# Another order of issue for a kernel that adds a long convolution and a gated unit, on one core

## The chip, the cores and the metric

One core of one Trainium2 chip. The metric is the device time in microseconds (us) of one execution, as the median of several runs. The core has five engines that run side by side, each through its own list of instructions in order: PE (TensorE, matmuls), DVE (VectorE), ACT (ScalarE), POOL (GpSimd) and SP (SyncE, which here only issues DMA transfers). An instruction waits until the results that it needs are there, and what stands behind it on its engine waits with it.

## What is computed

```python
x = A_q                                    # 2048 rows x 640 columns, bf16
xn = _layernorm(x, axis=-1)
return x + _A_ref(xn, A_k, A_v, A_shift_k, A_ssm_k, A_ssm_D) \
         + _B_ref(xn, B_w_gate, B_w_up, B_w_down)

# _A_ref(q, k, v, ...): a convolution over all 2048 rows
k_shift = sum of k_pad[:, t:t + S, :] * shift_k[:, 3 - t]   # four shifted copies of k
kv = k_shift * v
y = causal convolution of kv with ssm_k along the rows (by FFT), column by column
return q * (y + kv * ssm_D)

# _B_ref(x, ...): a gated unit, 640 -> 1728 -> 640
g, u = x @ w_gate, x @ w_up
return (sigmoid(g) * u) @ w_down
```

## The kernel before, in words

Two jobs share the engines.

**The gated unit** works on four tiles of 512 rows, numbered 0 to 3. A tile's normalised rows are turned (tile xnT; tiles 0 and 1 on PE, tiles 2 and 3 by a transposing DMA that reads them back from DRAM, `rec_tp`, L699). For each of 14 column groups fc of 128 columns, five matmuls of 128x512 make the gate and five the up half in PSUM (`rec_fc`, L770); ACT takes the sigmoid (L729, L735) and DVE multiplies (L732, L737) into hT; in some groups ACT copies the up half out first (L314, as hT<-g). Then `rec_down` multiplies hT with the down weights, seven matmuls of 128x320 at a time (L786), and DVE adds the result to the row accumulator acc (L798). Gate and up weights come in pieces called w3_0, w3_1 and so on (tile 3; even numbers gate, odd ones up, four column groups each, 640 KB) into four buffers; a piece can be loaded once the last matmul that reads the buffer's former piece is done (L378).

**The convolution** goes over the columns in two halves, each in five parts, so ten in all, as an FFT in matrix form. For a part, DVE makes kv (L470 to L488); stage 1 (L508, 32 small matmuls a group) and stage 2 (L528, 32 a group) transform on PE; ACT takes their results out of PSUM (L314, L317); DVE multiplies the spectra (`rec_prod`, L548 to L567; for seven of the parts two DMA transfers P<-S first swap the two halves of the partitions); stage 3 (L580, 8 matmuls a group) goes back into V. When five parts are done, stage 4 (`rec_st4`, L612) makes the half's rows, in four pairs u = 0 to 3 of two groups of 64 matmuls of 32x80; ACT or DVE evicts them, DVE multiplies them with the normalised rows, which a DMA has read back from DRAM into a buffer (L600; xq in half 0), and adds them to acc (L620, L621). Half 0 has two such buffers, so pair 2's rows are loaded when pair 1's addition is done. At the end SP stores acc in 24 transfers (L630).

The layer norm of tiles 1 to 3 is split: ACT makes sums and sums of squares (L646, L652), DVE the inverse root, ACT or DVE the rows (L685, L683).

**The order.** The program records 984 operations, each with what it reads and writes, and then emits them in the order of a list of numbers, `ORDER`; each engine's instruction list is what falls to it of that list. An operation that ACT and DVE can both do is done by ACT unless its number is in `ON_DVE`. Where a tile has several buffers, the order also decides which one it gets (`emit`). Nothing else sets the order.

The operations that the change and the prediction speak of, by number:

| Numbers | Operation |
|---|---|
| 384, 385; 377, 378; 391, 392; 398, 399 | stage 4 of half 0: the pairs u = 1, 0, 2, 3 |
| 579, 580; 572, 573; 586, 587; 593, 594 | stage 4 of half 1: the pairs u = 1, 0, 2, 3 |
| 388, 389 | DVE's product and addition of pair u = 1, half 0 |
| 390 | load of the rows for pair u = 2, half 0 |
| 437 | a DVE product of part 5 that waits for the transfers P<-S |
| 807, 841 | last up group of tile 2 that reads its xnT; the transposing load of tile 3 |
| 881, 893 | tile 3: gate of fc 3; up of fc 5 |
| 886, 887 | loads of the weights w3_2 and w3_3 |
| 45; 135, 136 | eviction of sT; norm of tile 1's rows, groups 2 and 3 |
| 139, 140, 141, 144 | norm of groups of rows of tiles 2 and 3 |
| 293; 820, 895 | eviction for the head of kt, half 1; copies of an up half to hT |
| 568, 570, 574, 575, 581, 582 | evictions of stages 3 and 4, half 1 |
| 960 to 967; 968 to 971; 972 to 983 | stores of rows 0 to 11; 12 and 13; 14 and 15 |

(Stores: in units of 128 rows.)

Of the kernel before, what the change touches and what calls it, by code (L numbers as in the profile page):

```python
# [42 lines left out]
def _dft_tables():  # L43
# [34 lines left out]


ORDER = [  # L80
    3, 5, 0, 8, 2, 7, 6, 42, 71, 12, 10, 13, 4, 11, 72, 14, 16, 1, 19, 73, 74, 75, 91, 76, 607, 86, 608, 18, 43, 96,
    77, 61, 97, 78, 79, 104, 62, 63, 64, 81, 20, 80, 92, 87, 17, 82, 98, 83, 643, 15, 88, 84, 85, 148, 99, 93, 89,
    645, 100, 149, 60, 625, 644, 58, 90, 94, 67, 626, 102, 101, 27, 150, 103, 613, 621, 66, 44, 615, 623, 65, 106, 68,
    154, 622, 57, 624, 614, 616, 617, 619, 105, 153, 609, 56, 59, 22, 611, 618, 108, 620, 599, 601, 610, 612, 600, 29,
    107, 109, 646, 602, 157, 32, 158, 648, 603, 605, 112, 647, 650, 113, 30, 151, 649, 651, 652, 635, 637, 111, 110,
    152, 604, 636, 31, 606, 638, 23, 155, 26, 631, 627, 633, 632, 25, 156, 24, 629, 118, 117, 634, 21, 639, 641, 120,
    628, 630, 640, 642, 667, 35, 114, 661, 116, 668, 671, 115, 662, 665, 121, 119, 36, 133, 122, 123, 127, 681, 124,
    673, 39, 37, 682, 128, 684, 674, 677, 134, 45, 129, 679, 135, 653, 680, 38, 654, 683, 663, 131, 657, 136, 658,
    664, 33, 47, 666, 125, 48, 675, 126, 137, 34, 54, 172, 655, 656, 676, 163, 678, 669, 164, 659, 162, 130, 660, 28,
    670, 165, 672, 689, 691, 167, 739, 741, 132, 166, 181, 690, 692, 168, 53, 740, 721, 182, 742, 831, 723, 743, 693,  # L90
    744, 159, 298, 160, 41, 171, 722, 745, 724, 698, 40, 161, 700, 730, 169, 49, 732, 699, 701, 702, 52, 183, 832,
    734, 731, 300, 50, 178, 51, 736, 170, 173, 733, 175, 179, 735, 180, 174, 685, 176, 737, 738, 138, 177, 195, 687,
    196, 725, 727, 299, 199, 305, 186, 185, 184, 201, 202, 197, 46, 686, 688, 187, 188, 198, 189, 200, 203, 301, 833,
    707, 709, 190, 791, 69, 192, 302, 55, 726, 712, 194, 728, 193, 708, 729, 141, 70, 710, 213, 227, 191, 714, 214,
    713, 711, 139, 303, 228, 715, 215, 95, 716, 703, 718, 229, 304, 218, 217, 233, 230, 204, 206, 231, 704, 140, 142,
    216, 219, 771, 705, 706, 220, 234, 221, 208, 694, 696, 224, 695, 232, 697, 205, 717, 226, 249, 254, 719, 753, 225,
    207, 143, 222, 746, 772, 755, 720, 250, 209, 251, 754, 210, 253, 223, 757, 756, 252, 211, 758, 767, 759, 260, 235,
    237, 239, 212, 255, 263, 760, 256, 768, 236, 238, 261, 262, 288, 264, 290, 763, 265, 266, 267, 269, 770, 270, 241,
    242, 257, 240, 243, 244, 258, 834, 268, 836, 747, 285, 407, 748, 146, 289, 306, 751, 245, 271, 273, 412, 275, 291,
    286, 786, 247, 788, 749, 259, 287, 761, 318, 272, 294, 145, 762, 246, 750, 319, 297, 248, 752, 320, 321, 764, 324,  # L100
    325, 410, 274, 322, 276, 279, 409, 765, 280, 292, 787, 323, 277, 278, 766, 315, 789, 769, 835, 293, 326, 838, 308,
    309, 837, 327, 295, 296, 317, 281, 307, 839, 840, 310, 777, 282, 790, 779, 811, 283, 316, 778, 312, 782, 284, 328,
    329, 340, 354, 330, 331, 784, 783, 780, 334, 785, 341, 144, 773, 332, 342, 812, 360, 358, 355, 333, 413, 356, 774,
    311, 792, 781, 359, 345, 775, 361, 776, 357, 336, 813, 313, 335, 822, 338, 362, 815, 824, 408, 337, 823, 314, 339,
    363, 825, 376, 793, 795, 344, 351, 353, 343, 346, 794, 411, 147, 796, 817, 404, 347, 352, 427, 814, 819, 365, 364,
    366, 826, 428, 406, 429, 431, 367, 418, 816, 370, 405, 433, 371, 432, 828, 867, 368, 414, 383, 818, 374, 434, 369,
    797, 820, 821, 375, 799, 372, 373, 827, 348, 349, 829, 350, 798, 830, 384, 385, 430, 417, 435, 800, 387, 416, 419,
    415, 806, 436, 866, 424, 801, 386, 425, 808, 802, 377, 426, 421, 378, 379, 380, 388, 389, 803, 449, 390, 804, 463,
    450, 420, 805, 464, 422, 807, 437, 453, 860, 809, 451, 381, 841, 810, 465, 467, 468, 423, 382, 469, 470, 439, 854,
    397, 861, 864, 438, 391, 392, 855, 440, 858, 872, 394, 452, 441, 466, 455, 874, 848, 456, 460, 454, 849, 852, 393,  # L110
    462, 443, 856, 442, 398, 399, 857, 461, 400, 444, 445, 859, 401, 471, 844, 457, 447, 458, 459, 472, 446, 448, 490,
    473, 842, 485, 486, 499, 500, 845, 847, 474, 843, 846, 487, 501, 503, 504, 476, 475, 477, 479, 505, 478, 850, 506,
    489, 862, 496, 502, 498, 480, 863, 851, 481, 865, 482, 507, 873, 508, 483, 886, 887, 488, 853, 491, 493, 877, 497,
    492, 494, 527, 875, 878, 876, 510, 512, 515, 484, 529, 528, 531, 533, 879, 880, 516, 509, 532, 881, 534, 511, 513,
    514, 883, 868, 519, 530, 870, 395, 882, 520, 926, 884, 535, 536, 571, 869, 521, 523, 927, 871, 901, 495, 903, 885,
    892, 537, 396, 928, 402, 522, 585, 894, 902, 906, 524, 904, 526, 592, 539, 578, 893, 525, 538, 517, 888, 549, 541,
    895, 896, 518, 905, 550, 890, 897, 551, 907, 555, 553, 899, 540, 898, 543, 544, 542, 900, 929, 556, 545, 554, 552,
    931, 930, 557, 558, 889, 932, 908, 403, 891, 559, 910, 547, 909, 911, 921, 561, 563, 912, 923, 922, 560, 914, 924,
    548, 913, 917, 546, 915, 564, 567, 562, 565, 566, 569, 933, 568, 570, 579, 580, 916, 925, 934, 919, 581, 582, 918,
    935, 583, 920, 572, 936, 584, 573, 574, 937, 940, 575, 586, 576, 577, 962, 587, 938, 589, 588, 590, 960, 942, 939,  # L120
    591, 967, 966, 593, 594, 941, 595, 963, 596, 944, 597, 598, 943, 945, 946, 947, 968, 948, 950, 971, 969, 949, 964,
    961, 952, 951, 965, 953, 975, 970, 972, 974, 973, 954, 955, 958, 979, 976, 956, 978, 977, 9, 957, 959, 980, 982,
    981, 983
]
ON_DVE = [
    101, 103, 133, 34, 140, 144, 820, 568, 582, 574, 589, 588, 595
]


# [798 lines left out]
```

## Time and profile before

| What | Value |
|---|---|
| Time of the kernel before, median of 3 runs | 256.01 us (255.62 to 257.51) |
| The profiled execution's own time | 256.55 us |
| Its span, from the first instruction to the last | 254.8 us |
| Granted TensorE clock | 0.998 |
| Matmuls of 128x512 (L770) | 520, 379 ns drawn for each |
| Matmuls of 128x320 (L786) | 448, 299 ns |
| Stage 4 (L612) | 1024, 203 ns |
| Idle of DVE before hT (L737), for PE | 17.7 us |
| Idle of ACT before sig (L735), for PE | 14.7 us |

A page of the profile gives each engine's busy time and its share of the span, then 40 equal slices of the span in which a digit is the busy share in tenths, then the DMA queues (packets, megabytes, share of the time of 16 DMA engines), the chain that ended last, and groups of instructions: line, engine, operation, out<-in, shape, count, busy us, mean ns of one, and the idle time ahead of them with what ended it. A timeline row has the start, the length, the engine, the line, the operation and the count, and in brackets the idle time before it and its releaser; "issue" is a wait for nothing that the profile shows. PEld are PE's weight loads, one for each matmul. Matmuls overlap, so the length drawn for one is longer than the step from one to the next.

### The profile page before, as it was taken

The page shows a single profiled execution, that of the slowest core. Times are in us where ns is not written, and L with a number is a line of the kernel's source. Part 1 is how long each engine was busy: PE and PEld are TensorE (multiplying, and loading weights), DVE is VectorE, ACT ScalarE, POOL GpSimd, SP SyncE. Part 2 cuts the span into 40 slices and gives each one's busy share as a digit, 9 for nine tenths or more (in the row PEclk, how much of TensorE's full clock was granted, in tenths as well). Part 3 has the DMA queues.
Part 4 walks back from the last instruction along what each step waited for, and adds up shares of the span by engine and source line. Part 5 has one row for each costly group of instructions (what it writes and reads, how often), then busy time and mean ns, then how long its engine had stood idle before and what let it go on. Part 6 is the DMA issues. An engine that isn't in the chain of part 4 may idle for free.

```text
span 254.8 us, 9455 instructions
## 1 busy us (share of the span) xinstructions
PE 241.0 (95%) x4231; PEld 145.1 (57%) x4231; DVE 199.8 (78%) x334; ACT 179.0 (70%) x263; POOL 0.7 (0%) x6
## 2 busy tenths in 40 slices
PE   7899999999999999999999999979999999898991
PEld 3654446664454657666564654656766465356770
DVE  5723347279999999999999999997999896878920
ACT  2737789975899986987798888846878895461300
POOL 1000000000000000000000000000000000000000
PEclk9999999999999999999999999999999999999999
DMA  6999999999989087698999757842127697000861
GB/s 179 335 250 317 246 256 135 143 184 192 153 196 290 5 227 187 95 144 118 166 226 234 194 163 190 100 111 59 35 55 233 148 300 214 3 3 23 191 156 53
DMA packets 91024, 41.44 MB, mean 163 GB/s; under 512 B 66656, under 2 KB 88104, under 8 KB 90664
## 3 DMA queue, kind: packets, MB, share of 16 engines
q1 hardware_dynamic: 90792, 40.52, 71.7%
q8 instruction: 33, 0.54, 0.9%
q10 hardware_dynamic: 192, 0.33, 0.4%
q14 instruction: 7, 0.06, 0.1%
HBM read 30.61 MB, written 5.24 MB: 141 GB/s over the span
## 4 chain that ended last, share of the span: by engine, by line
PE 59%; DVE 19%; ACT 9%; DMA 5%; issue 4%; ACTq 1%; SPq 0%; DVEq 0%
PE g L770 30%; PE g L786 16%; PE c L528 5%; DMA P<-S 3%; ACT jk L646 3%; PE c L612 3%; DVE kvt L488 2%; PE c L580 2%; DVE P L558 2%; ACT S L314 2%; DVE ta L475 2%; PE c L508 2%; DMA acc<-in_A_q_dram 2%; DVE tb L470 1%; PE c L750 1%
## 5 line engine op out<-in xcount | busy, mean ns | idle before, releaser
L770 PE MATMUL g<-xnT,w 128*128 128x512 bf16 x380 | 90.0, 379 | 0.9 <-DVE hT L737 0.7
L786 PE MATMUL g<-wd,hT 128*128 128x320 bf16 x448 | 66.6, 299 | 1.5 <-issue 0.8
L770 PEld LDWEIGHTS <-w 128*128 128x128 bf16 x380 | 35.0, 98 | 38.4 <-issue 1.2
L786 PEld LDWEIGHTS <-hT 128*128 128x128 bf16 x448 | 42.2, 98 | 19.0 <-issue 2.2
L314 ACT CAST S<-c 128x1024 bf16<-128x1024 f32 x40 | 39.7, 1027 | 3.9 <-PE c L528 3.8
L737 DVE TENSOR_TENSOR hT<-sig,g 128x512 bf16<-128x512 bf16 x32 | 21.9, 685 | 19.3 <-PE g L770 17.7
L770 PE MATMUL g<-xnT,V 128*128 128x512 bf16 x140 | 32.7, 379 | 0.0
L735 ACT ACTIVATE sig<-g 128x512 bf16<-128x512 f32 x32 | 19.3, 605 | 15.9 <-PE g L770 14.7
L798 DVE TENSOR_TENSOR acc<-g,acc 128x320 bf16<-128x320 f32 x32 | 15.5, 489 | 15.1 <-PE g L786 14.8
L528 PEld LDWEIGHTS <-Mt 64*128 64x128 f16 x1280 | 19.8, 95 | 5.4 <-issue 5.1
L314 ACT CAST T<-c 128x1024 bf16<-128x1024 f32 x20 | 19.8, 1020 | 3.6 <-PE c L508 3.5
L528 PE MATMUL c<-T,Mt 64*128 64x64 bf16 x1280 | 22.1, 190 | 0.0
L314 ACT CAST V<-c 128x1024 bf16<-128x1024 f32 x19 | 19.2, 1025 | 3.4 <-PE c L580 2.4
L488 DVE TENSOR_TENSOR kvt<-ta,vt 128x1024 bf16<-128x1024 bf16 x10 | 21.5, 2148 | 0.1
L770 PEld LDWEIGHTS <-V 128*128 128x128 bf16 x140 | 13.1, 98 | 14.7 <-issue 0.2
L317 ACT ACTIVATE T<-c 128x1024 bf16<-128x1024 f32 x20 | 20.3, 1039 | 0.8 <-PE c L508 0.8
L729 ACT ACTIVATE sig<-g 128x512 bf16<-128x512 f32 x18 | 10.9, 605 | 7.8 <-PE g L770 3.1
L475 DVE TENSOR_TENSOR ta<-ta,tb 128x1024 bf16<-128x1024 bf16 x20 | 13.8, 690 | 0.4
L470 DVE TENSOR_TENSOR tb<-kt,sT 128x1024 bf16<-128x1024 bf16 x20 | 13.7, 686 | 0.2
L561 DVE TENSOR_TENSOR S<-S 128x1024 bf16<-128x1024 bf16 x20 | 13.5, 687 | 0.3
L580 PEld LDWEIGHTS <-S 128*128 128x128 bf16 x160 | 10.9, 98 | 3.9 <-DVE S L567 1.2
L580 PE MATMUL c<-At,S 128*128 128x128 f16 x160 | 13.0, 219 | 0.0
(83 smaller groups left out, 241.2 us busy)
## 6 DMA issues: line engine op xcount, KB each, us to landing
w<-in_B_w_gate_dram SPq DMA_DIRECT2D x7, 640.0 KB, 5.7
w<-in_B_w_up_dram SPq DMA_DIRECT2D x7, 640.0 KB, 4.6
P<-S SPq DMA_DIRECT2D x14, 256.0 KB, 3.9
kt<-in_A_k_dram SPq DMA_DIRECT2D x8, 320.0 KB, 6.6
vt<-in_A_v_dram SPq DMA_DIRECT2D x8, 320.0 KB, 5.5
xnd<-xq SPq DMA_DIRECT2D x4, 640.0 KB, 4.7
ht<-in_A_ssm_k_dram SPq DMA_DIRECT2D x16, 96.0 KB, 4.3
wd<-in_B_w_down_dram SPq DMA_DIRECT2D x3, 480.0 KB, 8.6
```

Source lines behind the costliest of these rows:

```text
L314: fa = lambda: nc.scalar.copy(out=out_fn(), in_=in_fn())
L317: fa = lambda: nc.scalar.activation(out_fn(), in_fn(), ACT.Copy, scale=scale)
L470: dve(1024, 2, lambda: nc.vector.tensor_tensor(tl[c][:], sl(tl[kb], 3 - m), sh(m), ALU.mult) if c != o else nc.vector.tensor_tensor(tl[c]. ...
L475: dve(1024, 2, lambda: nc.vector.tensor_tensor(tl[a][:], tl[a][:], tl[c][:] if c != o else tl[c].rearrange("p b n j -> p n b j"), ALU.add) ...
L488: dve(1024, 1 if kt else 2, lambda: nc.vector.tensor_tensor(by_j(tl[o]) if kt else tl[o][:], tl[a].rearrange(form), sl(tl[vb], 0).rearrang ...
L528: nc.tensor.matmul(tl[c][:, b, 64 * kk:64 * kk + 64], lhsT=Mb[rows, k, 64 - 64 * r:192 - 64 * r], rhs=tl[T][rows, 2 * k + r].rearrange("p ...
L580: nc.tensor.matmul(o, lhsT=tl[S_][:, b, 0, j, :], rhs=Ab[:, 2 if zc else 0, :], start=True, stop=zc)
L735: act(512, lambda: nc.scalar.activation(tl[sg][:], pv(0), ACT.Sigmoid), r=[pk(0)], w=[(sg,)], alloc=[(sg, "sig")], pri=pri - 2000)
L737: dve(512, 1, lambda: nc.vector.tensor_tensor(hT[:, fc, :], tl[sg][:], pv(1), ALU.mult), r=[pk(1), (sg,)], w=[(hk, fc)], pri=pri - 2000)
L770: nc.tensor.matmul(tl[c][:], lhsT=w()[:, k, o:o + P], rhs=tl[X][:, k, :], start=(k == 0), stop=(k == NC - 1))
L786: nc.tensor.matmul(tl[pd[i]][:, 0:320], lhsT=hT[:, fc, t4 * P:(t4 + 1) * P], rhs=wd[:, fc, 320 * i:320 * i + 320], start=(fc == 0), stop=( ...
L798: dve(320, 1, lambda i=i, m=m, pd=pd: nc.vector.tensor_tensor(acc[:, m, 320 * i:320 * i + 320], tl[pd[i]][:, 0:320], acc[:, m, 320 * i:320 ...
```

## The change

Only the two lists change. The same 984 operations are issued in another order, and some operations change between ACT and DVE: 45, 135, 136, 139, 141, 293, 570, 575, 581 and 895 go to DVE; 140, 144, 568, 574, 582 and 820 go to ACT. The order came out of a search in which an engine's instruction fetch waits until the block ahead has come.

Nearly every line of `ORDER` differs; these are the ones around the operations in the table above.

```diff
 ORDER = [
...
-    797, 820, 821, 375, 799, 372, 373, 827, 348, 349, 829, 350, 798, 830, 384, 385, 430, 417, 435, 800, 387, 416, 419,
-    415, 806, 436, 866, 424, 801, 386, 425, 808, 802, 377, 426, 421, 378, 379, 380, 388, 389, 803, 449, 390, 804, 463,
-    450, 420, 805, 464, 422, 807, 437, 453, 860, 809, 451, 381, 841, 810, 465, 467, 468, 423, 382, 469, 470, 439, 854,
-    397, 861, 864, 438, 391, 392, 855, 440, 858, 872, 394, 452, 441, 466, 455, 874, 848, 456, 460, 454, 849, 852, 393,
-    462, 443, 856, 442, 398, 399, 857, 461, 400, 444, 445, 859, 401, 471, 844, 457, 447, 458, 459, 472, 446, 448, 490,
...
-    489, 862, 496, 502, 498, 480, 863, 851, 481, 865, 482, 507, 873, 508, 483, 886, 887, 488, 853, 491, 493, 877, 497,
-    492, 494, 527, 875, 878, 876, 510, 512, 515, 484, 529, 528, 531, 533, 879, 880, 516, 509, 532, 881, 534, 511, 513,
...
-    961, 952, 951, 965, 953, 975, 970, 972, 974, 973, 954, 955, 958, 979, 976, 956, 978, 977, 9, 957, 959, 980, 982,
...
+    797, 821, 828, 384, 430, 347, 349, 866, 385, 435, 799, 408, 350, 418, 387, 798, 827, 800, 386, 436, 424, 886, 416,
+    829, 806, 802, 426, 830, 417, 377, 388, 425, 463, 801, 415, 808, 804, 464, 437, 378, 389, 438, 380, 803, 439, 379,
+    805, 390, 449, 419, 807, 841, 450, 441, 854, 421, 391, 381, 392, 420, 809, 810, 440, 382, 443, 860, 855, 442, 393,
+    861, 451, 394, 467, 468, 858, 864, 422, 453, 397, 469, 470, 465, 423, 444, 868, 870, 850, 398, 452, 455, 399, 466,
...
+    873, 498, 865, 875, 869, 521, 510, 522, 527, 493, 877, 528, 876, 871, 509, 523, 881, 887, 883, 533, 529, 534, 879,
+    512, 492, 531, 878, 511, 513, 530, 515, 514, 516, 532, 880, 892, 494, 495, 882, 535, 536, 894, 517, 884, 893, 907,
...
+    971, 970, 949, 952, 968, 951, 953, 973, 975, 956, 974, 957, 972, 959, 981, 954, 955, 958, 982, 983, 980, 979, 976,
...
 ON_DVE = [
-    101, 103, 133, 34, 140, 144, 820, 568, 582, 574, 589, 588, 595
+    101, 103, 45, 133, 136, 135, 34, 139, 141, 293, 895, 570, 581, 575, 588, 589, 595
 ]
```

## The prediction

> **What bounds the kernel now.** I read the page first, then the groups by shape, then the order of PE's instructions, and last the timeline around PE's gaps. From the page, and from the groups by shape (the last line):
>
> ```profile
> span 254.8 us, 9455 instructions
> ...
> PE 241.0 (95%) x4231; PEld 145.1 (57%) x4231; DVE 199.8 (78%) x334; ACT 179.0 (70%) x263; POOL 0.7 (0%) x6
> ...
> PE   7899999999999999999999999979999999898991
> ...
> DVE  5723347279999999999999999997999896878920
> ...
> q8 instruction: 33, 0.54, 0.9%
> ```
> ```profile
> L612 PE MATMUL c<-V,Bt 32*32 32x80 bf16 x1024 | 10.6, 203 | 2.1 <-issue 2.1
> ```
>
> PE is busy in nearly every slice from 10 to 249 us, so the time is PE's work plus PE's waits, with DVE close behind (91.25 of the 94 us from 56 to 150). Queue 8 carried 33 packets, 0.54 MB: 16.4 KB each. PE has 8462 instructions (a weight load and a matmul, 4231 of each): 256 to a packet, 64 bytes each. So PE's program comes in blocks of 256. Stage 4 (L612) is densest: 128 instructions in about 0.63 us. There PE waits for "issue". The timeline, engine PE:
>
> ```profile
> 151.58 1.34 PE L612 MATMUL c<-V,Bt 32*32 32x80 bf16 x128
> ...
> 155.57 0.86 PE L612 MATMUL c<-V,Bt 32*32 32x80 bf16 x84
> 157.00 0.52 PE L612 MATMUL c<-V,Bt 32*32 32x80 bf16 x44 [0.56 <-issue]
> ```
> ```profile
> 165.20 0.27 PE L612 MATMUL c<-V,Bt 32*32 32x80 bf16 x20
> 166.21 1.06 PE L612 MATMUL c<-V,Bt 32*32 32x80 bf16 x108 [0.74 <-issue]
> ...
> 171.21 0.41 PE L508 MATMUL c<-Ft,kvt 32*128 32x64 f16 x32 [0.86 <-ACT xq L314]
> ...
> 174.94 0.54 PE L612 MATMUL c<-V,Bt 32*32 32x80 bf16 x46 [0.53 <-issue]
> ```
> ```profile
> 229.85 0.99 PE L786 MATMUL g<-wd,hT 128*128 128x320 bf16 x6 [0.83 <-issue]
> ...
> 233.30 0.80 PE L612 MATMUL c<-V,Bt 32*32 32x80 bf16 x77 [0.27 <-issue]
> ```
>
> Counted in PE's instructions these six stand at 4532, 5042, 5296, 5552, 7600 and 7856, all 176 to 180 past a multiple of 256, in the middle of groups whose data were there: block edges. (The 0.86 is put down to ACT, but its place is the same.) The idle adds up to 3.8 us. A shown end includes some 0.2 us of pipeline (a matmul is drawn 203 ns long while 64 of them start within 0.63), so the loss is 3.8 + 6 x 0.18 = 4.9 us. Between waits that follow each other lie 171.21 to 174.94 = 3.73 us and 229.85 to 233.30 = 3.45 us: the least time of a block. From 166.21 to 171.21 it was 5.0, with the transposing load of tile 3's rows in flight. The counter-example is the first line above: instructions 4020 to 4276, one whole block and nearly all stage 4, passed with a wait of 0.1 us; their packet ran from 150.37 to 151.44, before they were reached, because two L770 groups of 1.08 us stood ahead.
>
> **The change part by part.** Same operations, same buffers. Sums are made in the profiled execution, 256.55 us (span 254.8); the median of the runs is 256.01, and differences carry over.
>
> *Fetches.* With block edges at the same counts, the new order puts stage 4's pairs of half 0 at 4004-4260 (as before), 4364-4492 plus 4556-4684 (split), 4782-5038 and 5296-5552: the last two each fill one block. Laying the rows end to end (L770 1.08, L786 0.95, L528 0.47, L508 0.34, L612 0.63, 0.1 at each change of form) the blocks hold, in us:
> - 4276-4532 and 4532-4787: 4.3 and 4.6, over 3.73: 0.1 lost (0 to 0.7), where before lost 0.75.
> - 4787-5042: 1.3 of stage 4 alone. At best the stream is ahead by the L770 and L786 groups in front (2.0), and the edge at 5042 costs 3.45 - 3.3 = 0.1. At worst it is not ahead and the transposing load is in flight: 5.0 - 1.3 = 3.7. That load is issued after the last tile-2 L770 group, 14 instructions before this block, so I take 2.4, nearer the worst. Before: 0.92 + 1.02 at these two edges.
> - 5296-5552: the same shape, but 6.4 us of work lie before it and that load has landed: 0.2 (0.1 to 2.4). Before 0.7.
> - The last three (7344 on): 3.3, 3.05, 3.05 against 2.7, 3.0, 3.95 before: 1.0 (0.95 to 1.8). Before 1.45.
>
> Sum 3.7 (1.15 to 8.6) against 4.9: **-1.2** (-3.75 to +3.7).
>
> *Changes of form.* L508, L528 and L612 come in 41 runs instead of 43; each costs 0.1 going in and out: **-0.4**.
>
> *ACT to DVE at 45-50 us.* sT's eviction and two norms of tile 1 go to DVE. PE waited there: one L786 group starts at 48.18, the next at 49.69, 0.56 over its 0.95. ACT was full (9.78 of 40-50), DVE half empty (5.01) with 1.7 to 2.3 us idle between evictions, which hides 0.82 + 2 x 0.44; uncovered, that would be 1.7. **-0.5** (-0.56 to 0). In the full DVE stretch the exchanges cancel: two norms in (0.88), two out (0.88), kt's head in (0.40), one hT copy out (0.69).
>
> *Stores.* SP issues its last stores back to back:
>
> ```profile
> 241.84 10.78 SPq L630 DMA_DIRECT2D out_dram<-acc  x19
> ```
>
> 0.57 us each, up to 252.6, and the span ends 2.2 later. One store of rows 12-13 now goes ahead of the last twelve: **-0.5** (-1.3 to 0).
>
> *What gets later.* (a) Stage 4's third pair starts about 4 us earlier and needs a row load that two DVE operations release; one of them now stands behind a product that waits for the P<-S load. In before the load landed 8.8 us after the first pair's end; the new order gives 10.35 us of PE work, less what DVE loses: **+0.5** (0 to 1.5). (b) The weights w3_3 were issued at 190.06, long before use. Now their buffer is free only when the L770 group of fc 3 (gate) ends, 5.2 us of PE work ahead of their first use by fc 5 (up). The weight loads' line has
>
> ```profile
> DMA to landing us min/median/max: 4.5/5.3/9.2
> ```
>
> so 0.2 to issue plus 5.3, less 5.2: **+0.3** (0; 3.3 at the 8.3 us that this load took beside its twin). The wait at 218.99 (0.69, for an hT product that stands behind the P<-S load on DVE) stays; its order there is the same.
>
> Sum: -1.2 - 0.4 - 0.5 - 0.5 + 0.5 + 0.3 = -1.8: 254.75 in the profiled execution, **254.2** from the median.
>
> **The rivals.**
>
> *The filled blocks run free.* As 4020-4276 did, if the stream keeps its lead: loss 1.15 instead of 3.7, 254.2 - 2.55 = 251.6. For it: the two pairs fit their blocks to within six instructions. Against it: the transposing load.
>
> *The fetch is no limit, so nothing is won there.* If the six waits are queue waits that merely show up there, they move along: 254.2 + 1.2 = 255.4. Against it: six of six at one remainder. [...]
>
> *No lead (slower).* Where the stream reaches a stage-4 block only as PE does, its 1.3 us cover nothing: 3.7 at 5042, 2.4 at 5552, the other ends with them, 8.6 in all: 254.2 + 4.9 = 259.1. It ends above before once the two blocks cost 4.4 together instead of 2.6. For it: the block ahead, 4.6 us, is under the 5.0 seen with a load in flight, and could use up the lead.
>
> *w3_3 lands late.* At 8.3 us, 254.2 + 3.0 = 257.2; it decides from a landing of 7.1. Against it: nothing else is issued beside it.
>
> **How the numbers follow.** The forecast 0.44, free blocks 0.28, no limit 0.10, no lead 0.10, w3_3 late 0.08. 254.2 is the likeliest's; its own range is 253.0 to 255.6, from the ends of its small terms. The range 251.4 to 257.4 takes in free blocks and late weights and leaves out no lead and the far edge of free blocks. A measurement of this kernel tells about 1% (2.6 us) from no change: faster by more than that is free blocks and a little of the forecast, 0.34; slower is most of no lead and a little of late weights, 0.12; within it 0.54.
>
> **What would show it.** PE's waits for issue: none in the split pair (4364-4684), one of 2 us or more just after the pair at 4782-5038, next to none after 5296-5552, three small ones after 228 us. ACT's wait of 0.39 at 49.69 gone. PE's wait for w at the first fc 5 (up) group under 0.5. The last store's issue half a us nearer to PE's end. I am wrong if PE's waits for DVE or ACT grow by over 1 us between 56 and 150, where DVE has 2.7 us to spare, or if the edges have moved.

## The result, and the profile after

The changed kernel takes **256.28 us** (median of 20 runs, 253.32 to 258.92) where the kernel before, run beside it, takes 257.37 us (median of 20). The ratio is **0.9935, 95% interval 0.9908 to 0.9961**: 0.4 to 0.9% faster. (The ratio is formed from the fast runs alone and leaves out six of the changed kernel's 20, 257.25 to 258.92 us with a mean clock of 0.986 to 0.993; that is why the medians of all 20 lie only 1.1 us apart.) In a second series the medians were 254.38 us (12 runs) and 256.21 us (23 runs), ratio 0.9925 (0.9897 to 0.9953). The execution that was profiled was the slowest of the 20 (258.92 us, with PE's clock at half speed for a while), so times of it are not compared with those of before as they stand.

Its page:

```profile
span 257.1 us, 9426 instructions
...
PE 241.5 (94%) x4199; PEld 146.9 (57%) x4231; DVE 202.2 (79%) x338; ACT 177.0 (69%) x259; POOL 0.7 (0%) x6
...
PE   7999999999999999999999899599989999899993
...
PEclk9999999999999999999999999869999999999999
...
q8 instruction: 33, 0.54, 1.0%
```

PE's row has a hole in the 26th slice (163 to 166 us), and the clock's row, full in the kernel before, dips in the slices 26 and 27. (32 of the 4231 matmuls are missing from this record; the weight loads are complete.) The timeline of the changed kernel, engine PE, shows the hole: stage 4's pair u = 2 (128 matmuls of L612) and what follows.

```profile
161.82 1.23 PE L612 MATMUL c<-V,Bt 32*32 32x80 bf16 x128
162.98 0.31 PE L786 MATMUL g<-wd,hT 128*128 128x320 bf16 x1
166.43 5.37 PE L786 MATMUL g<-wd,hT 128*128 128x320 bf16 x20 [3.15 <-issue]
```

The pair runs without a stop, one matmul of the next group starts, and then PE stands for 3.15 us for nothing that the profile shows: this is PE instruction 5040, a block edge. The 20 matmuls behind it take 5.37 us; the same 20 take 2.89 us where the clock is whole (below). The table by stretches of the same profile (the column behind POOL is the granted clock) says why:

```profile
160.00:163.00 3.00, 3.00 (x141) 1.99 (x139) 2.93 (x5) 1.43 (x2) 0.00 (x0) 1.00 0.47 131
163.00:166.40 3.40, 0.28 (x7) 0.07 (x1) 3.33 (x7) 2.20 (x3) 0.00 (x0) 0.75 1.17 121
166.40:168.00 1.60, 1.57 (x6) 0.88 (x7) 0.54 (x1) 0.00 (x0) 0.00 (x0) 0.50 1.03 263
```

The clock falls to 0.50 while PE waits and stays there for 6.8 us in all. The edges behind 228 us answer to those of before at 229.85 and 233.30: one visible wait, in the middle of a stage-4 group.

```profile
239.95 0.30 PE L612 MATMUL c<-V,Bt 32*32 32x80 bf16 x29
240.88 0.98 PE L612 MATMUL c<-V,Bt 32*32 32x80 bf16 x99 [0.63 <-issue]
```

At the end, SP's 24 stores, first in the kernel before and then in the changed one:

```profile
234.66 17.96 SPq L630 DMA_DIRECT2D out_dram<-acc  x24
```
```profile
237.45 17.50 SPq L630 DMA_DIRECT2D out_dram<-acc  x24
```

They end at 254.95 us, 2.27 us behind PE's last matmul (252.68). In the kernel before they ended at 252.62, 3.58 us behind PE's end at 249.04. From PE's end to the end of the span it was 5.71 us and is now 4.40 us.

### The profile page after: what moved, and what is told of

It is laid out like the page before. It is cut to its first block, busy times and chain, and to the rows that moved or that the text cites. A ratio compares the mean times of both kernels' runs of the same rounds, so it can differ in the third digit from the quotient of the medians.

```text
span 257.1 us, 9426 instructions
## 1 busy us (share of the span) xinstructions
PE 241.5 (94%) x4199; PEld 146.9 (57%) x4231; DVE 202.2 (79%) x338; ACT 177.0 (69%) x259; POOL 0.7 (0%) x6
## 4 chain that ended last, share of the span: by engine, by line
PE 50%; DVE 31%; DMA 8%; issue 4%; ACT 4%; SPq 1%; DVEq 0%; ACTq 0%
PE g L770 24%; PE g L786 15%; DMA P<-S 6%; DVE kvt L488 4%; DVE ta L475 4%; DVE P L558 3%; DVE S L561 3%; DVE S L565 3%; PE c L816 3%; ACT S L314 2%; PE c L612 2%; DVE S L567 2%; DVE acc L798 2%; DMA ht<-in_A_ssm_k_dram 2%; DVE tb L470 2%
## 5 line engine op out<-in xcount | busy, mean ns | idle before, releaser
L770 PE MATMUL g<-xnT,w 128*128 128x512 bf16 x355 | 88.1, 379 | 3.4 <-DVE hT L737 1.0
L786 PE MATMUL g<-wd,hT 128*128 128x320 bf16 x448 | 68.4, 307 | 3.5 <-issue 3.1
L786 PEld LDWEIGHTS <-hT 128*128 128x128 bf16 x448 | 43.4, 100 | 22.7 <-issue 4.1
L567 DVE TENSOR_TENSOR S<-P 64x1024 bf16<-64x1024 bf16 x18 | 12.4, 689 | 0.6
L565 DVE TENSOR_TENSOR S<-S 64x1024 bf16<-64x1024 bf16 x18 | 12.4, 687 | 0.6
```

Source lines behind the costliest of these rows:

```text
L565: dve(n, 2, lambda b=b: nc.vector.tensor_tensor(X(b)[0:64], X(b)[0:64], X(b)[64:P], ALU.subtract), r=[(S_, "p", b)], w=[(S_, "z", b)], pri ...
L770: nc.tensor.matmul(tl[c][:], lhsT=w()[:, k, o:o + P], rhs=tl[X][:, k, :], start=(k == 0), stop=(k == NC - 1))
L786: nc.tensor.matmul(tl[pd[i]][:, 0:320], lhsT=hT[:, fc, t4 * P:(t4 + 1) * P], rhs=wd[:, fc, 320 * i:320 * i + 320], start=(fc == 0), stop=( ...
```

## The experiments

The theory: PE's program comes in blocks of 256 instructions, each block takes at least about 3.5 us to arrive (3.45 and 3.73 us between two waits of the kernel before), and where a block holds less work than that PE stands at its edge; the change gathers several such waits into one, behind pair u = 2. The rivals: the waits belong to operations (queues, data), not to places in the program; or the transposing load's traffic makes them. "Loss" below is the step from one matmul's start to the next, less the shortest step seen between two matmuls of those shapes.

**1. The changed kernel again.** No edit.

> The changed kernel once more, to see its profile apart from the one run. Theory (instruction fetch): the wait of 3.2 us right behind stage 4's pair u = 2 (PE instruction 5042) comes back in every execution, since it hangs on the place of the block edge; 2.4 to 3.4 us. The half-speed clock behind it, 6.8 us long in the first profile, is a consequence that comes or stays away with the length of the wait. Time 253.5 to 257.5 us. Rival (a disturbance of that one execution, or a wait for data): under 1.5 us there this time.

Measured: 254.38 us (252.56 to 258.38). The profiled execution was again the longest (258.38 us), with the same wait at the same instruction, and the clock again at 0.50 behind it:

```profile
165.82 5.51 PE L786 MATMUL g<-wd,hT 128*128 128x320 bf16 x20 [3.09 <-issue]
```

So it is no single accident. But it is not in every execution either: kernels 6, 7, 11 and 12 below have the changed kernel's order up to here, and stood 1.33, 1.03, 1.13 and 1.11 us. The theory's 2.4 to 3.4 us in every execution is wrong: the place is fixed, the length is 1.0 to 1.3 or 3.1.

**2. Pair u = 2 taken apart.**

```diff
-    ..., 391, 381, 392, 420, 809, 810, 440, 382, 443, 860, 855, 442, ...
+    ..., 391, 381, 420, 809, 810, 440, 382, 443, 860, 855, 392, 442, ...
```

> The changed kernel with the second group of pair u = 2 of half 0 moved behind 24 other PE instructions (a gate group of L770 and a down group of L786, about 2 us of work), so that the pair no longer fills one block. Theory (fetch): the wait of 3.2 us at the edge falls to 0.1 to 1.5 us, and no half-speed clock follows; 1.5 to 5 us faster than the changed kernel, 250.5 to 253. Rival (the wait belongs to the operation behind the pair, through a queue or data): it stays at the same operation with its length, and the time is within 1 us of the changed kernel's.

Measured: 255.27 us, ratio to before 0.9968 (0.9941 to 0.9995); no gain on the changed kernel. (What came to stand between the pair's two groups is two down groups, 14 matmuls.)

```profile
161.47 0.69 PE L611 MATMUL c<-V,Bt 32*32 32x80 bf16 x64
162.09 1.12 PE L785 MATMUL g<-wd,hT 128*128 128x320 bf16 x7
164.15 1.12 PE L785 MATMUL g<-wd,hT 128*128 128x320 bf16 x7 [0.94 <-DVE hT L731]
...
173.18 0.19 PE L611 MATMUL c<-V,Bt 32*32 32x80 bf16 x1 [1.04 <-issue]
```

The wait at the edge is gone, as the theory says. Two others stand in its place: the group moved ahead needs an hT product that DVE finishes at that moment (0.94), and the next pair's edge (5550) now costs 1.04. The product is that of the second down group behind the pair, so in the changed kernel the edge hides only a part of this wait: in kernel 11, with no fetch to wait for, PE would be through the first group at about 163.8 (162.83 plus 0.95) and could begin the second when DVE's product ends, at 164.25, and with the fetch wait it begins it at about 165.1. By this estimate a wait of 1.13 us at the edge costs some 0.8. Kernel 2 loses at its tail too: the edge 8110 costs a wait of 1.73 us, and the clock is at 0.50 for 3.4 us behind it.

**3 and 4. All edges moved, no operation moved.** Three of the first twelve warm-up matmuls are replaced by 87 tiny ones, 168 more PE instructions, in the kernel before (3) and in the changed one (4).

```diff
-    plan.op({"PE": (4.4, lambda: warm(12))}, ...
+    plan.op({"PE": (4.4, lambda: (warm(9), warm_small(87)))}, ...
```

> The kernel before with three of its first twelve warm-up matmuls replaced by 87 tiny ones (168 more PE instructions in about the same time, at the very start); no operation after that is moved, but every block edge falls 168 instructions earlier among the operations. Theory (fetch): the six waits leave their places (4532, 5042, 5296, 5552, 7600, 7856 of the old count) for places 168 earlier or 88 later, and as stage 4's pairs now lie worse against the edges, their sum grows from 4.9 to 7 to 11 us: 258.5 to 262. Rival (queue or data waits): same operations, same waits, time within 1 us of the kernel before (256 to 257).

> The changed kernel with the same 168 additional PE instructions at the start and nothing else. Theory (fetch): pair u = 2 now straddles an edge (its last 82 instructions stand behind it), the 3.2 us wait behind it goes, and the fetch loss falls from about 4.5 us to 1.5 to 3; no half-speed clock; 1 to 4 us faster than the changed kernel. Rival (queue or data waits): the wait stays behind pair u = 2 and the time is within 1 us of the changed kernel's. Were only the additional matmuls to matter, this kernel and the shifted one before would both be slower or faster by the same.

Measured: 265.57 us (ratio 1.0373, 1.0342 to 1.0403) for the kernel before, and 262.06 us (median of six runs that lie apart, one at 257.03 and five at 261.57 to 263.02, so that no ratio was formed) for the changed one. The tiny matmuls were not free: they took 4.82 us, the next seven warm-ups 3.18 instead of 1.67, and PE reached its first L786 group 5.28 us later in the one and 5.78 us later in the other. Less that, kernel 3 is 4.1 us slower than the kernel before; 1.5 us of this are two waits for weight loads (at 142 and 146 us) that the kernel before does not have, and the loss at the edges is 7.7 us, where the theory forecast 7 to 11. Kernel 4, less the same, is 3.1 us faster than the changed kernel by its one short run and 1.9 us slower by its median, so its time decides nothing. PE's waits in the shifted kernel before:

```profile
166.98 1.68 PE L770 MATMUL g<-xnT,w 128*128 128x512 bf16 x5 [3.54 <-issue]
177.92 0.69 PE L612 MATMUL c<-V,Bt 32*32 32x80 bf16 x64 [1.02 <-issue]
...
242.94 0.42 PE L612 MATMUL c<-V,Bt 32*32 32x80 bf16 x33 [1.34 <-issue]
247.76 0.61 PE L612 MATMUL c<-V,Bt 32*32 32x80 bf16 x54 [0.74 <-issue]
```

and in the shifted changed kernel:

```profile
165.34 0.42 PE L612 MATMUL c<-V,Bt 32*32 32x80 bf16 x33 [2.22 <-issue]
175.01 1.22 PE L528 MATMUL c<-T,Mt 64*128 64x64 bf16 x72 [0.96 <-issue]
...
243.23 0.61 PE L612 MATMUL c<-V,Bt 32*32 32x80 bf16 x55 [1.62 <-issue]
```

They stand at the instructions 4788, 5298, 8112, 8368 and 4786, 5296, 8366: 174 to 180 past a multiple of 256, as ever, and in front of other operations than before. This rules out that they belong to operations. In kernel 4 pair u = 2 is freed as forecast, but the split pair, which ran without a stop, now shares one block and pays 2.22 us, and the loss at the edges is 5.7 us, where the theory forecast 1.5 to 3.

**5. No transposing load.** Tile 3 of the gated unit is computed from tile 2's rows (that part of the output is not the reference's).

```diff
-    plan.op({"SP": (4.5, lambda: nc.sync.dma_start(tl[X][:], ..., transpose=True))},
+    plan.op({"SP": (4.5, lambda: tr > 2 or nc.sync.dma_start(tl[X][:], ..., transpose=True))},
...
+        if b == "xnT3":
+            return tl["xnT2"]
```

> The changed kernel without the transposing load of tile 3's rows: tile 3 of the gated unit is computed from tile 2's rows, so the last quarter of its output is not the reference's. Theory (no lead plus traffic): the fetch for the block behind pair u = 2 starts only when PE enters the pair's own block, so the wait stays at 3.45 (least time of a block) less 1.3 (the pair's work) = 2.0 to 2.3 us, and only the 1.1 us above that goes with the load. Rival (the load's traffic is all of it): 0 to 0.5 us. Rival (traffic plays no part): 3.0 to 3.4 us as before. Time 1 to 3 us under the changed kernel by the first, 3 to 5 by the second, within 1 us by the third.

Measured: 253.85 us, ratio to before 0.9925 (0.989 to 0.996), the changed kernel's own. The wait at 5040:

```profile
164.06 2.89 PE L788 MATMUL g<-wd,hT 128*128 128x320 bf16 x20 [0.81 <-issue]
```

Under the first forecast and the third, over the second: none has it. The fetch packet for that block started at 161.74, just as PE entered the pair (161.78), and PE went on 2.3 us behind the packet's start; the theory had put the full 3.45 us there. (The 0.81 is no wait for the hT product of kernel 2: PE goes on at 164.06, and that product ends at 164.40.) With the load, the packet started at 162.15 and 161.70 in kernels 7 and 11 (waits 1.03 and 1.13), but at 163.41 and 163.89 in the two executions with waits over 3 us. So with the load in flight the packet is 2 us late in some executions and not in others. What decides is not shown: in all four PE entered the pair 0.85 us behind the issue of the load. Nor does one profile without the load show that the load is the cause. In the medians, with intervals of some 0.9 us either way, the load costs nothing that shows.

**6 and 12. Blocks alone.** Idle work behind the changed kernel's last matmul. In 6 the small matmuls all use one quadrant of the array; in 12 they are spread over the 16 as stage 4's are.

```diff
+    for _ in range(1024):
+        nc.tensor.matmul(wz[0:32, 0, 0:80], lhsT=ident[0:32, 0:32], rhs=ident[0:32, 0:80], start=True, stop=True)
...
+    tiny(1024)
+    wide(64, 320)
+    wide(512, 48)
```

> The changed kernel with idle work behind its last matmul: 1024 matmuls of 32x80 in stage 4's shape (8 blocks of 256 instructions), 64 matmuls of 128x320, 512 matmuls of 128x64 and 512 of 128x96; most of it runs when no data transfer is in flight. Theory (fetch): among the 1024, PE stands about 2.2 us at every 256th instruction, 3.4 to 3.7 us from wait to wait, some 28 us in all; the matmuls of 128x64 (some 3.5 us of work in a block) hardly wait, those of 128x96 not at all. Rival (a limit in how PE issues small matmuls, or in queues): no wait at the edges, 8 blocks in 10 to 12 us. On the clock: if a wait of 2.2 us in every 3.5 us is enough to lower it, it is at 0.5 there and the first 128x320 steps take 0.27 us instead of 0.14; if only waits over 3 us do that, it stays at 1.0.

> The changed kernel with idle work behind its last matmul, with hardly a transfer in flight: (A) 1024 matmuls in stage 4's very form, spread over the array's 16 quadrants as there (8 blocks of 256 instructions), then 64 of 128x320, (B) 512 of 128x48, 64 of 128x320, and (C) 16 rounds of 64 as in stage 4 and 14 of 128x320. Theory (fetch): in A PE stands at each block edge, 3.3 to 3.7 us from one to the next, 27 to 30 us for the eight; in B (2.8 us of work) it stands 0.6 to 0.9 us at each edge; in C (6 us of work in a block) not at all. Rival (small matmuls are slow to issue): no stops at the edges in A, 10 to 13 us. On the clock: A has 1.3 us of small matmuls and 2.2 us of waiting in every 3.5 us, and if both count as idle, the clock is 0.5 through A and the first 128x320 behind it take 0.27 us; if only single waits over 3 us count, it is 1.0. In B and C it is 1.0.

Measured in 6: in one quadrant the 1024 follow each other at 36 ns at first and at 66 to 67 ns once the clock has fallen to 0.50, 4.6 and 8.5 us to a block, so no edge could show. The 128x64 matmuls took 29 ns each, 3.7 us to a block, with no step over 30 ns at any edge. In 12, the timeline of PE behind the kernel's own work:

```profile
248.54 1.89 PE L904 MATMUL c<-hT,ident 32*32 32x80 bf16 x208
252.46 1.30 PE L904 MATMUL c<-hT,ident 32*32 32x80 bf16 x128 [2.03 <-issue]
256.19 1.30 PE L904 MATMUL c<-hT,ident 32*32 32x80 bf16 x128 [2.42 <-issue]
260.19 1.31 PE L904 MATMUL c<-hT,ident 32*32 32x80 bf16 x128 [2.70 <-issue]
...
275.38 0.63 PE L904 MATMUL c<-hT,ident 32*32 32x80 bf16 x48 [2.42 <-issue]
```

Seven stops, one after every 128th matmul (256 instructions), at instructions 174 past a multiple of 256, 3.73 to 4.0 us apart, with hardly a transfer in flight and no data to wait for. That is the theory by itself: a block with 1.3 us of work takes 3.7 us and more here. B had no stops, where the theory forecast 0.6 to 0.9 us at each edge: at 25 ns each, its 128x48 matmuls are 3.2 us of work in a block, not the 2.8 assumed. Its packets started 3.36 to 3.80 us apart while PE crossed the edges 3.20 apart, so the stream fell about 1 us behind in B, and a lead of that size must have covered it. In none of the profiles here do two of PE's packets start less than 3.26 us apart (behind the first 20 us): that is the least time of a block seen here. C had no stops either. The clock, in the same profile:

```profile
248.00:252.00 4.00, 2.44 (x213) 1.97 (x212) 0.49 (x1) 0.00 (x0) 0.00 (x0) 0.95 0.14 35
252.00:256.00 4.00, 1.30 (x128) 1.12 (x128) 0.00 (x0) 0.00 (x0) 0.00 (x0) 0.50 0.06 14
```

It is at half speed through A from the first stop on, with no single wait over 2.7 us of idle.

**7. The tail spread.** Down groups drawn forward between the last stage-4 groups, and the eviction 588 moved from DVE to ACT; the order of the stores as in the changed kernel.

```diff
-    572, 573, 575, 574, 576, 577, 963, 938, 937, 961, 940, 586, 587, 588, 589, 590, 591, 964, 942, 939, 941, 593, 594, ...
+    572, 938, 937, 573, 575, 574, 576, 577, 963, 940, 939, 961, 586, 942, 587, 588, 589, 941, 590, 591, 964, 943, 593, ...
```

> The changed kernel with the down groups (L786) of its last 12 us drawn forward between the stage-4 groups of half 1, so that each of the last three blocks with stage 4 in it holds 3.4 to 4.4 us of work instead of 3.0 to 3.3; one eviction (588) goes from DVE to ACT. Theory (fetch): the three edges' loss falls from 1.3 (2.9 where stores collide with a fetch) to 0.2 to 0.8 us: 0.5 to 2 us faster than the changed kernel. Rival (DVE, which has under 0.5 us idle between 228 and 244 us, sets the pace there): the waits for issue become waits for DVE's additions into acc, and the time stays within 0.5 us.

Measured: 258.32 us, ratio 1.009 (1.0056 to 1.0124). The stops for issue behind 228 us are gone, and PE waits longer for DVE:

```profile
235.02 1.11 PE L785 MATMUL g<-wd,hT 128*128 128x320 bf16 x7 [1.48 <-DVE acc L797]
...
243.26 8.07 PE L785 MATMUL g<-wd,hT 128*128 128x320 bf16 x56 [2.20 <-DVE acc L797]
```

The rival's mechanism, and worse than it said: drawn forward, the down groups hold PSUM buffers that DVE, busy with stage 4's evictions, products and additions, frees late.

**8. One and two down groups inside the pairs u = 2 and u = 3.**

```diff
-    ..., 854, 421, 391, 381, 392, ...            868, 870, 850, 398, 452, 455, 399, 466, 400, 471, 472, 401, 851, 853, ...
+    ..., 421, 391, 854, 381, 392, ...            868, 870, 398, 850, 851, 452, 455, 399, 466, 400, 471, 472, 401, 853, ...
```

> The changed kernel with one down group moved between the two groups of pair u = 2 and two down groups between those of pair u = 3 (half 0): no other order is touched. Theory (fetch): block 4784 to 5040 holds 2.2 us of work instead of 1.3, so the wait at 5040 falls from 3.2 to 2.0 to 2.5 us and block 5296 to 5552 (3.1 instead of 1.3) costs at most 0.5; the half-speed clock is rarer; 0.5 to 2.5 us faster than the changed kernel. Rival (the wait belongs to what stands behind the pair, whose data come at that moment): the wait at 5040 ends at the same time as before with the same operation, and the time is within 0.5 us.

Measured: 255.35 us, ratio 0.9975 (0.9944 to 1.0006); no gain.

```profile
164.40 2.89 PE L785 MATMUL g<-wd,hT 128*128 128x320 bf16 x20 [1.19 <-issue]
```

A wait of 1.19 us, and no half-speed clock. But that is as long as in kernels 6, 7, 11 and 12 (1.03 to 1.33), whose pair is whole, so the profile does not show that the work put into the block helped. The edge 8110 behind 235 us costs 2.0 us here, in an order that is the changed kernel's there.

**9. The order of the stores alone**, in the kernel before.

```diff
-    ..., 962, ..., 960, ..., 967, 966, ..., 963, ..., 968, ..., 971, 969, ..., 964, 961, ..., 965, ..., 975, 970, ...
+    ..., 962, ..., 960, 963, 961, ..., 967, 966, 964, 965, ..., 968, ..., 971, 969, 970, ..., 975, ...
```

> The kernel before with SP's stores alone in another order, close to the changed kernel's: 963, 961, 964, 965 and 970 are drawn forward, so that all stores of rows 0 to 13 go ahead of the twelve of rows 14 and 15; nothing else moves. From the end of PE's last matmul to the end of the span the kernel before takes 5.8 us, the changed one 4.4. Theory (SP's queue of stores was the end's limit): 4.4 to 4.7 us here, and 1.0 to 1.4 us faster than before; that is most of what the change brings. Rival (the end is set by PE's last results alone, the queue hides): 5.5 us or more and within 0.4 us of before.

Measured: 255.48 us against 256.30, ratio 0.9973 (0.9947 to 1.0).

```profile
234.36 16.72 SPq L629 DMA_DIRECT2D out_dram<-acc  x24
```

From PE's end (248.82) to the end of the span (253.2) it takes 4.39 us, the changed kernel's 4.40, where before had 5.71. The theory's 1.3 us are there in the profile; the time agrees with it (0.8 less, interval 0 to 1.4).

**10. Three operations on DVE alone**, in the kernel before.

```diff
-    101, 103, 133, 34, 140, 144, ...
+    101, 103, 45, 133, 136, 135, 34, 140, 144, ...
```

> The kernel before with the operations 45, 135 and 136 alone on DVE instead of ACT. Theory (ACT held PE up at 49.69 us): PE's 0.39 us wait for ACT there is gone, PE is 0.5 us earlier behind it, and 0.2 to 0.5 us of that are left at the end. Rival (DVE or the next wait takes it back before 60 us): the wait goes but PE is as late as before at the next L508 group, time unchanged. Rival (DVE is late instead): a wait for DVE of 0.3 us or more in the same place.

Measured: 256.34 us, ratio 0.9997 (0.9973 to 1.0021). The wait for ACT is gone, the two groups run on:

```profile
48.25 2.06 PE L786 MATMUL g<-wd,hT 128*128 128x320 bf16 x14
```

PE's loss between 25 and 50 us fell from 0.71 to 0.15 us, and nothing came in its place up to 100 us. In the time it does not show; an effect of 0.5 us is inside the interval. Whether it reaches the end stays open.

**11. No stores of rows 0 to 11**, in the changed kernel (those rows are not written).

```diff
-            dma(lambda e, q=q: e.dma_start(oq4[q][:, m0:m1, d0:d1], ...
+            dma(lambda e, q=q: m0 < 12 or e.dma_start(oq4[q][:, m0:m1, d0:d1], ...
```

> The changed kernel without the eight stores of rows 0 to 11 (those rows of the output are not written). In the profiles in which PE came early to its tail, the wait at edge 8110 was 1.7 to 2.0 us, and the block's fetch started 2.6 to 2.8 us after PE entered the block ahead instead of 0.9 to 1.1, some 2 us after the first two stores were issued. Theory (the stores' data hold the fetch up): the fetch starts at 0.8 to 1.3 us, the wait at 8110 is 0.3 to 0.6, and the time is 1 to 2.5 us under the changed kernel's. Rival (the fetch is late of itself): the wait stays over 1.5 us, and the time moves by under 0.7 us.

Measured: 254.37 us, ratio 0.9923 (0.9891 to 0.9954), the changed kernel's.

```profile
164.27 2.89 PE L786 MATMUL g<-wd,hT 128*128 128x320 bf16 x20 [1.13 <-issue]
...
236.35 0.98 PE L612 MATMUL c<-V,Bt 32*32 32x80 bf16 x99 [0.63 <-issue]
```

In this profile the fetch for edge 8110 started 1.12 us after the block's entry, and the wait was 0.63 us, where kernels 2, 6 and 8 (fetch 2.6 to 2.8 us after the entry) stood 1.73 to 2.00. But the time did not fall as forecast, and that the stores are what holds the fetch up is not shown. Kernel 12 has all of them, issued as long after the block's entry as in kernel 8, and its wait there is half as long:

```profile
236.81 0.98 PE L612 MATMUL c<-V,Bt 32*32 32x80 bf16 x99 [0.90 <-issue]
```

Kernel 5 (0.91) and the two profiles of the changed kernel (0.63 and 0.36) have short waits with the stores as well.

## Why the prediction was right in its sum and wrong in its terms

The forecast of 254.2 us was before's 256.01 less 1.8, a ratio of 0.993; measured 0.9935 and 0.9925. The terms, one by one, show that the sum came out by luck: the gains forecast and found are not the same ones.

- **Fetches, -1.2: not borne out.** Added up over the edges, the order before lost 4.85, 3.94 and 3.54 us (profiles of before, 9 and 10); the changed one lost 4.4, 4.4 and 2.6 (kernel 1, and the changed kernel's own part of 6 and 12). The means are 4.1 and 3.8, and the scatter is over 1 us on both sides. Two steps were wrong. The 4.9 us of before were taken from one execution, as if an edge had one price; it varies by over 1 us. And the 2.4 us put on the block of pair u = 2 were a middle between two values that occur, 1.0 to 1.5 (kernels 5 to 8, 11 and 12) and 3.3 (the two profiles of the changed kernel). Of the other parts, the split pair has no wait, and pair u = 3 costs 0.05 to 0.3 in the changed kernel (0.2 forecast). The last edges (1.0 forecast) cost 1.1 to 1.2 in its two profiles and 1.3 in kernel 12, but 2.7 to 2.9 in kernels 2, 6 and 8, which have its order there.
- **The half-speed clock: not in the sum at all.** In the two profiles of the changed kernel, with waits of 3.15 and 3.09 us, it costs 2.5 and 2.6 us (20 matmuls in 5.37 and 5.51 us instead of 2.89; a step of 0.267 us in the first instead of 0.136), on top of the wait. Over the 20 runs: nine with a mean clock of 0.993 or less have a median of 257.3 us, the eleven above it 254.7. The 2.6 us between them are about half of the spread of 253.3 to 258.9.
- **Changes of form, -0.4**: the shortest steps of all pairs of shapes add up to 0.3 us less. About right, too small to see.
- **ACT to DVE, -0.5**: right in its place (kernel 10: 0.56 us less loss, no substitute), not shown in the time.
- **Stores, -0.5: mis-sized, -1.3.** The prediction counted one store that goes ahead of the last twelve, at 0.57 us; that figure is a mean that holds SP's waits too, and stores issued back to back start 0.4 to 0.5 us apart. Before, SP issued its last eight stores back to back from 249.0 on, while PE had ended at 249.04: the queue was late by more than one issue, since the stores of rows 0 to 11 were put behind ones that waited for later results. In the changed kernel each of the last groups of four is issued as its rows are done. Kernel 9 shows it by itself in the profile.
- **(a) +0.5 and (b) +0.3: nothing.** The load of the rows for pair u = 2 was issued at 158.71, 3.1 us before the pair, which started without a wait. The weights w3_3 were issued at 200.02, 10 us later than before, and no matmul waited for them.
- **What was not in the sum: waits for DVE and ACT.** Away from the edges PE lost about 1.7 us between 50 and 175 us before, and about 3.2 in kernel 1 and 3.4 in kernel 11. The biggest: a gate group behind stage 2 at 142 us that waits for an hT product (0.18 to 1.2 idle), and a group of L508 at 153 us for kvt (0.42). The prediction's own limit, "over 1 us between 56 and 150", was nearly reached: PE's idle for DVE and ACT there was 0.2 us before, and 0.6, 1.0, 1.2, 0.9 and 0.9 in the changed kernel and in kernels 1, 6, 11 and 12.

So what is shown of the gain is 1.3 us at the end, by the stores; on PE what it wins at one place it gives back at another, and in executions with the half-speed clock it gives back more. What stays open: where the rest of the 1.7 to 1.9 us comes from, and what a run of 253 us does at the edges. The two profiled executions of the changed kernel were the longest of their 20 and 12 runs; only kernel 12, with 2.6 us at the edges, hints at a shorter one. The rival that the fetch is no limit is refuted (kernels 3, 4, 12), but its result, that nothing is won there, is close to what was seen.

No experiment gave a kernel clearly faster than the changed one.

## What to carry to other kernels

Here a stretch of small matmuls was limited by the arrival of its instructions (3.3 to 4.0 us for 256): in kernel 12 a block with 1.3 us of work took 3.7 us and more, and where slower work shared the block (C, 78 matmuls in 2.63 us, so 4.3 us for 256 instructions) there was no stop. So look what slower work shares the block of a dense group. One long wait cost the clock too (0.50 for 6.8 us with the wait of 3.15 us). Before a wait is removed, look what is ready behind it: here, with the wait at the edge gone, PE stood 0.94 us for a product of DVE (kernel 2), and the tail belonged to DVE (kernel 7). A term that rests on one execution's waits needs a second profile of the same kernel, and the issue queue of the final stores a look of its own.

## What was not expected of the hardware

**The clock was at half speed for multiples of 3.41 us.** In the changed kernel's profile it is 0.50 for 6.83 us, in kernel 2 for 3.41, in kernel 12 for 27.3 and in kernel 6 for 64.9: 2, 1, 8 and 19 times 3.41 us. 6.8 us at half speed in 255 us is a mean of 0.987, and half as long 0.993; of the changed kernel's 20 runs one shows 0.986 and six show 0.993. In kernel 12 it stayed at 0.50 for 27 us through waits of 2.0 to 2.7 us with 1.3 us of 32x32 matmuls between them, and in kernel 6 through small matmuls in one quadrant without any wait. That stage 4's own 1.3 us have a part in the fall behind pair u = 2, beside the wait of 3.15 us, is a guess from these two; no run shows it for that place. The same kind of wait does not always do it: behind edge 8110 the clock fell in kernel 2 (1.73 us) and not in kernels 6 and 8 (2.00 us each).

**A fetch came 1.7 us later in one execution than in another**, with a large transfer in flight in both: the same packet started at 162.15 us in kernel 7 and at 163.89 in the changed kernel, where PE had entered the block ahead at 161.87 and 161.82. The transfer is longer then too: the transposing load took 6.6 us to land in the two profiles of the changed order with the late packet (after and kernel 1), and 4.9 to 5.8 in kernels 2, 6, 7, 8, 11 and 12. Which of the two delays the other is not shown.
